# A recurrent attention and two MoE layers on one core: the first two chunks in a new order

## The chip, the cores and the metric

The kernel runs on one core of a Trainium2 chip. The metric is the device time of one execution in microseconds (us), taken as the median of several runs. TensorE is PE in the profile, VectorE DVE, ScalarE ACT, GpSimd POOL, and SP is the engine that issues the DMAs.

## The reference

The input is a recurrent attention with 4 x 8 heads, 768 steps and head size 40. For every step t and head, with a 40 x 40 state S:

```
y[t] = r[t] @ S
S    = S * w[t][:, None] - outer(S @ a[t], b[t]) + outer(v[t], k[t])
```

The result, 3072 tokens of 320, goes through two feed-forward layers: MoE 1 is `h = x @ w_in` (320 x 2048), `g = h * clip(h + 3, 0, 6) / 6`, `g @ w_out`; MoE 2 is `((x @ w_a) * (x @ w_b)) @ w_out` with 1536 columns. The MoE weights arrive as 64-bit floats, which the kernel converts to 32 bits on the chip.

## The kernel before, in words

**Attention** is done in 12 chunks of 64 steps, all 32 heads at once. A chunk j has a fixed chain. `prep_w`, `prep_kb` and `prep_a` scale the inputs by running products of w (a scan and a reciprocal per quarter, DVE). `op_a` forms the products of the chunk on PE. GpSimd then inverts small 32 x 32 triangles: `t_load` writes them to DRAM (`scr`) and fetches them as TA2 (`TA`), `t_start` does 31 elimination steps of two instructions (L517, L520) into TL, and `t_store` lets ACT turn TL into `tnt` (L528) and sends TL and tnt through DRAM (`n`) back as NY and into AB. From there PE goes on: `merge_y` (L547), `merge_z` (L559), `op_c` and `op_d`, `op_e`, `op_g`, `op_f`, which gives Y; Y goes through DRAM to `xt`, the input of MoE 1 for this chunk. ACT copies what PE leaves in PSUM, in four banks, after each of these.

**MoE 1** for a chunk is a `prep` (ACT casts xt to xh, L288, DVE takes the rest xl) and 16 steps, up 0 to 7 and down 0 to 7. An up is 16 matmuls (L309), then ACT relu into the tile g (L314), DVE multiply (L315), ACT cast gh (L130), DVE rest gl (L131). A down is 12 matmuls (L329 to L331). MoE 2 follows when all chunks are done and keeps PE busy to the end.

**The order** on every engine is the order in which the Python program issues the work. Each chunk j has a window: a list of attention steps of chunk j and preparations of chunks j + 1 and j + 2, and between them places where one MoE 1 step (`MOE_STEP`) or one weight conversion (`WEIGHT`) goes; the places are the index lists MOE and WEIGHTS. A step issues its instructions on all engines, its DMAs on SP's queue among them.

**The weights** of MoE 1 come in 34 pieces (18 of w_in, 16 of w_out, in the order in which up and down need them). A conversion is: DMA into a tile, one ACT scaling (L77), five DVE instructions (L78 to L86), one ACT cast (L261), one DVE subtraction (L263). While room is wide (four tiles, xt, xh, xl and GH, are lent to the conversion), `Interleaved.round` overlaps three pieces, each round takes one new piece. `op_e` takes GH back, with extra rounds until GH is free; the first `xt_move` ends the wide state with `flush`. After that a piece goes through alone, from tiles `ws` and `cv`; an up or down whose weights are not there converts them first (`need`).

**Before the windows** a prologue prepares chunks 0 and 1, runs `t_start(0)` and `t_start(1)` on GpSimd, some conversions, the transposes `turn(0)` and `turn(1)`, and `t_store(0)`. `prep_kb` of chunk 1 is on GpSimd there, ahead of `t_start(0)`, and the second half of `t_load(1)` (the fetch into TA2, which GpSimd must have finished reading) stands on SP's queue ahead of the loads of chunk 2 and of `t_store(0)`.

The tail after the windows runs what is left of MoE 1, two steps apart, and converts the first 15 pieces of MoE 2's weights between them, one after each step from the third on.

Of the kernel before, what the change touches and what calls it, by code (L numbers as in the profile page):

```python
# [21 lines left out]
NCH = S // C  # L22
# [14 lines left out]
WEIGHTS = {
    0: (0, 3, 6, 8, 10, 17, 18, 21, 22, 22, 26, 27),
    1: (1, 2, 4, 5, 10, 13, 16, 16, 33, 36)}
STORE_1 = 25  # L40
WEIGHTS_2, RANGE = 2, 7
# [53 lines left out]
def attention_and_moe(ctx, tc, t, flag):  # L95
# [44 lines left out]
    def words(src, dma):  # L140
        st = wk1.tile([128, 192, 2], I32, tag="ws", name="ws", bufs=3)[:, 0:src.shape[1]]
        dma.dma_start(out=st.rearrange("q c w -> q (c w)"), in_=src.bitcast(I32))
        return st

    def from_words(st):
        cv = wk1.tile([128, 2, 192], I32, tag="cv", name="cv2", bufs=2)[:, :, 0:st.shape[1]]
        return to_f32(nc, st, cv[:, 0], cv[:, 1], st[:, :, 1])

    class Converter:
# [5 lines left out]
        def ahead(self, most=2):  # L155
            while self.todo and len(self.loaded) < most:
                k, src, n, sink, c0 = self.todo.pop(0)
                w, begun = self.load(src, n, sink, c0)
                if w < n:
                    self.todo.insert(0, (k, src[:, w:n], n - w, sink, c0 + w))  # L160
                self.loaded.append((k, begun))

# [12 lines left out]
    class Interleaved(Converter):  # L175


        x = y = z = None

# [3 lines left out]
        def go(self, n=1):  # L183
            if not room["wide"]:
                return super().go(n)
            for _ in range(n):
                self.ahead()
                self.round()
                self.ahead()
# [30 lines left out]
    def load1(src, n, sink, c0):  # L220

        slot = None
        if room["wide"]:
            slot = room["free"].pop(0)
            room["live"].add(slot)
            if slot == "GH":
                st = GH.rearrange("q a p c -> q (a p c)")[:, 0:2 * n]
                sp.dma_start(out=st if not wide else st.bitcast(I32), in_=src.bitcast(I32) if wide else src)
                st = st.bitcast(I32).rearrange("q (c w) -> q c w", w=2) if wide else st
            else:  # L230
                st = stage_load(wk1, (slot, 0, 0, 0, 0, 1), src, n, sp)
        else:
            n = min(n, 192)
            st = words(src[:, 0:n], sp) if wide else stage_load(wk1, ("ws", 0, 0, 0, 0, 3), src[:, 0:n], n, sp)

        def steps():
            if not wide:
                yield from range(6)
                w = st
            elif slot:  # L240
                room["n"] += 1
                h = wk1.tile([128, n], I32, tag=("cv", "gh")[room["n"] % 2], name="cv_h", bufs=2)
                f32_steps(nc, st, h, h, h)[0]()
# [12 lines left out]
            yield  # L256
        return n, steps()

    def weight_pieces1():
# [32 lines left out]
    def moe1_stream(j):  # L292
# [5 lines left out]
        def up(i):  # L298
            conv1.need(0, (2 * i + 1) // 3)
            xh, xl = stt["x"]  # L300
# [62 lines left out]
    TLs = [a1.tile([128, 32, 16], F32, name=f"TL{i}") for i in range(2)]  # L363
    TT2 = a1.tile([128, 256], F32, name="TT2")
    KBTv = [x[:, 0:2 * NP * D].rearrange("q (a p d) -> q a p d", a=2, p=NP) for x in KBTs]
# [13 lines left out]
    def setup_first():  # L379
        for q, eng in ((32, ve), (96, gp)):  # L380
            eng.memset(raw[q:q + 32], 1.0)
            eng.memset(raw[q:q + 32].rearrange("q (p t) -> q p t", p=NP)[:, :, 0:1], 0.0)
        load_kb(0)
# [110 lines left out]

    def t_load(j, between=lambda: None):
        scr = dram.tile([2, 2, NP, 32, 32], F32, tag="scr", name="scr", bufs=2)
# [6 lines left out]
        between()  # L503
        for h in range(2):
            sp.dma_start(out=TA2[half(h)], in_=scr.rearrange("u a p s t -> (u a p) s t"))

# [14 lines left out]

    def t_store(j, between=lambda: None):
        TL = TLs[j % 2]
        tnt = wk1.tile([128, 16, 32], F32, tag="g", name="tnt", bufs=1)
        NY = py["NY"] = a2.tile([128, NP, 32], F32, tag="py", name="NY")
        n1 = dram.tile([2, 2, NP, 32, 32], F32, tag="n1", name="n1", bufs=2)
        z, AB = n2[j % 2], ABs[j % 2]
        ac.copy(out=tnt, in_=TL.rearrange("q t c -> q c t"))  # L528
        for h in range(2):
# [3 lines left out]
            sp.dma_start(out=z.rearrange("a p (c h) t -> (a p) c h t", h=2)[:, :, h, 32:64], in_=tnt[r + 32:r + 64])  # L533
        between()
# [160 lines left out]
    WEIGHT, MOE_STEP = "weight", "moe"  # L695

    def window(j):

# [9 lines left out]
        def pk(*ks):  # L708
# [3 lines left out]
            [(op_b, j, 0), (op_b, j, 1)]  # L712
            + on(nx2 and j, (load_w, j + 2)) + on(nx2, (load_a, j + 2)) + on(j > 1, (t_store, j))
            + on(ahead, (op_a, j + 1, 0), (idle,))
            + on(ahead, (op_a, j + 1, 1), (idle,), (t_load, j + 1), (t_start, j + 1)) + pw(0)
            + on(ahead, (op_kbt, j + 1, 0), (op_kbt, j + 1, 1)) + pw(1)
# [8 lines left out]
            + on(nx2, (prep_a, j + 2, gp), (prep_sq, j + 2)))  # L725
        if j < 2:
            steps = [x for x in steps if x is not WEIGHT]
        out = []
        for i, x in enumerate(steps + [None]):
            if j == 0 and i == STORE_1:  # L730
                out.append((t_store, 1, conv1.go))
            if j == 1 and i == 0:
                out.append((xt_move, 0))
            out += [WEIGHT] * WEIGHTS.get(j, ()).count(i) + [MOE_STEP] * MOE[j].count(i)
            if x is not None:
                out.append(x)
# [178 lines left out]
    with tc.manual_schedule():  # L915
# [4 lines left out]
        for k in range(4):  # L920
# [51 lines left out]

        for j in range(NCH):
            for f in window(j):
                if f == MOE_STEP:
# [253 lines left out]
```

## Time and profile before

| | |
|---|---|
| median of 3 runs | 1327.77 us (1323.69 to 1331.85) |
| profiled execution | 1324.79 us, its span 1323.0 us |
| mean granted PE clock | 0.940 |
| busy | PE 84%, DVE 58%, ACT 38%, POOL 28% |
| DMA | 97.59 MB, mean 74 GB/s |

A share is of the whole span. The span has three stages: up to about 200 us the preparation, chunk 0 and the conversions, with PE mostly idle; then one window after another, with MoE 1 steps between attention steps; from about 908 us MoE 2.

### The profile page before, as it was taken

How to read it: one execution, taken by the hardware profiler on the slowest of the kernel's cores; microseconds unless marked ns; L12 is line 12 of the kernel's file. 1: busy time of each engine (PE TensorE's matmuls, PEld its weight loads, DVE VectorE, ACT ScalarE, POOL GpSimd, SP SyncE). 2: the span in 40 equal slices, each digit the busy share in tenths (PEclk: the TensorE clock that was granted, in tenths of full speed). 3: DMA queues.
4: the chain of work that ended last, by engine and by line, in shares of the span. 5: the costliest groups of instructions: out<-in, count | busy, mean ns of one | idle time of the engine just before them, and what ended most of it. 6: DMA issues, size and time to landing. Idle time of an engine off the chain costs nothing.

```text
span 1323.0 us, 34883 instructions
## 1 busy us (share of the span) xinstructions
PE 1110.3 (84%) x14826; PEld 1013.2 (77%) x14826; DVE 771.6 (58%) x1371; ACT 504.5 (38%) x1087; POOL 375.0 (28%) x829
## 2 busy tenths in 40 slices
PE   1314438898989898989999999877999999999998
PEld 1214338798989898988988898866888888888886
DVE  7869777374646556473746243576665675675333
ACT  2224244344444544354544534233433332332221
POOL 4775007171817263553627250000000000000000
PEclk9999658998989898989999899989999999999999
DMA  6245351424151524333241412122220110110011
GB/s 174 70 119 129 95 130 49 100 63 119 39 140 36 122 60 98 83 86 91 66 112 51 100 40 54 62 75 89 85 70 27 35 42 27 34 43 11 32 41 50
DMA packets 166403, 97.59 MB, mean 74 GB/s; under 512 B 124672, under 2 KB 155520, under 8 KB 164224
## 3 DMA queue, kind: packets, MB, share of 16 engines
q1 hardware_dynamic: 166240, 95.29, 27.9%
q8 instruction: 118, 1.93, 0.6%
q14 instruction: 45, 0.37, 0.1%
HBM read 75.33 MB, written 19.92 MB: 72 GB/s over the span
## 4 chain that ended last, share of the span: by engine, by line
PE 63%; DVE 9%; ACT 9%; DMA 7%; POOL 5%; issue 4%; SPq 4%; ACTq 0%; DVEq 0%; POOLq 0%
PE att L847 20%; PE up L309 10%; PE dn L329 4%; PE dn L331 3%; PE dn L330 3%; PE ac L871 3%; PE ac L870 3%; PE ac L869 3%; POOL TL L520 2%; POOL TT L517 2%; DMA n<-tnt 2%; PE att L614 2%; PE att L637 2%; PE att L631 2%; PE att L588 2%
## 5 line engine op out<-in xcount | busy, mean ns | idle before, releaser
L517 POOL TENSOR_TENSOR TT<-TA,TL 128x126 f32<-128x126 f32 (+22 forms) x372 | 146.3, 393 | 340.1 <-DMA TA<-scr 311.8
L847 PE MATMUL att<-x2h,up 128*128 128x512 f32 x720 | 237.2, 394 | 0.2 <-ACT x2h L831 0.2
L847 PE MATMUL att<-x2l,up 128*128 128x512 f32 x432 | 170.4, 394 | 1.9 <-DVE x2l L832 1.9
L520 POOL TENSOR_TENSOR TL<-TL,TT 128x126 f32<-128x126 f32 (+22 forms) x372 | 156.8, 421 | 29.1
L315 DVE SCALAR_TENSOR_TENSOR up<-g,up 128x512 f32<-128x512 f32 x96 | 66.4, 691 | 156.3 <-ACT g L314 156.3
L847 PEld LDWEIGHTS att<-x2h,up 128*128 128x128 f32 x720 | 135.0, 188 | 29.2 <-ACT x2h L831 0.5
L329 PE MATMUL dn<-wo_h,gh 128*128 128x320 f32 x384 | 137.2, 357 | 21.0 <-ACT gh L130 21.0
L314 ACT ACTIVATE g<-up,bias 128x512 f32<-128x512 f32 x96 | 66.3, 691 | 192.6 <-PE up L309 126.5
L331 PE MATMUL dn<-wo_h,gl 128*128 128x320 f32 x384 | 128.9, 336 | 1.4 <-DVE gl L131 1.4
L330 PE MATMUL dn<-wo_l,gh 128*128 128x320 f32 x384 | 128.0, 333 | 0.0
L309 PE MATMUL up<-xh,wi_h 128*128 128x256 f32 x384 | 107.2, 301 | 3.1 <-ACT xh L288 3.1
L852 DVE TENSOR_TENSOR att<-att,asb 128x512 f32<-128x512 f32 x72 | 50.4, 700 | 97.9 <-PE att L847 79.3
L131 DVE TENSOR_TENSOR gl<-up,gh 128x512 fp32r<-128x512 f32 x96 | 66.4, 692 | 65.9 <-ACT gh L130 65.9
L309 PE MATMUL up<-xh,wi_l 128*128 128x256 f32 x384 | 101.7, 286 | 0.0
L329 PEld LDWEIGHTS dn<-wo_h,gh 128*128 128x128 f32 x384 | 80.8, 210 | 26.6 <-ACT gh L130 22.9
L130 ACT CAST gh<-up 128x512 fp32r<-128x512 f32 x96 | 56.3, 586 | 114.8 <-DVE up L315 110.8
L847 PEld LDWEIGHTS att<-x2l,up 128*128 128x128 f32 x432 | 81.0, 188 | 19.4 <-DVE x2l L832 3.5
L869 PE MATMUL ac<-dn,g2h 128*128 128x320 f32 x288 | 89.5, 311 | 0.0
L871 PE MATMUL ac<-dn,g2l 128*128 128x320 f32 x288 | 88.6, 308 | 0.1
L870 PE MATMUL ac<-dn,g2h 128*128 128x320 f32 x288 | 88.7, 308 | 0.0
L449 DVE RECIPROCAL rw<-W 128x256 f32<-128x256 f32 x48 | 84.2, 1753 | 4.3 <-ACT sq L459 1.7
L331 PEld LDWEIGHTS dn<-wo_h,gl 128*128 128x128 f32 x384 | 80.6, 210 | 4.0 <-DVE gl L131 4.0
(146 smaller groups left out, 2411.9 us busy)
## 6 DMA issues: line engine op xcount, KB each, us to landing
RV<-in_rve_dram SPq DMA_DIRECT2D x24, 320.0 KB
KB<-in_kbe_dram SPq DMA_DIRECT2D x22, 320.0 KB
TA<-scr SPq DMA_DIRECT2D x24, 256.0 KB
st<-in_w1i_dram SPq DMA_DIRECT2D x13, 384.0 KB
raw<-in_we_dram SPq DMA_DIRECT2D x24, 162.5 KB
LB<-in_ae_dram SPq DMA_DIRECT2D x24, 160.0 KB
VX<-in_vte_dram SPq DMA_DIRECT2D x24, 160.0 KB
yt<-Y SPq DMA_DIRECT2D x48, 80.0 KB
```

Source lines behind the costliest of these rows:

```text
L131: eng.tensor_tensor(out=lo, in0=src, in1=hi.bitcast(F32), op=ALU.subtract)
L309: mm(u[:, e], a_, b_, start=(n == 0), stop=(n == len(seq) - 1))
L329: mm(acc, gh[:, e, c0:c0 + 128], wo_h[:, m], start=(m == 0), stop=False)
L330: mm(acc, gh[:, e, c0:c0 + 128], wo_l[:, m], start=False, stop=False)
L331: mm(acc, gl[:, e, c0:c0 + 128], wo_h[:, m], start=False, stop=(m == 15))
L449: ve.reciprocal(out=rw, in_=w[:, :, 1:65])
L517: gp.tensor_tensor(out=tv, in0=TA2[:, u:u + 1, u + 1:32].rearrange("q a t -> q t a").to_broadcast([128, m, n]), in1=TL[:, u:u + 1, 0:n].to ...
L520: gp.tensor_tensor(out=TL[:, u + 1:32, 0:n], in0=TL[:, u + 1:32, 0:n], in1=tv, op=ALU.subtract)
L847: mm(u, a_, b_, start=(n == 0), stop=(n == len(seq) - 1))
L869: mm(acc, gh[:, sl], w[:, 0], start=(i == 0), stop=False)
L870: mm(acc, gh[:, sl], w[:, 1], start=False, stop=False)
L871: mm(acc, gl[:, sl], w[:, 0], start=False, stop=(i == BLOCK - 1))
```

## The change

Tables MOE and WEIGHTS lose their entries for windows 0 and 1, which are now written out by hand in `first_windows`; windows 2 to 11 keep their places. `t_load` and `t_store` are each cut in two. `t_start(0)` is issued right after `setup_rest`, `prep_kb` of chunk 1 goes to DVE, the prologue has six conversion rounds, two of them in each `turn`, where it had fourteen, and the fetch of chunk 1's triangles comes after `t_store(0)`. `tnt` is no longer the tile g of MoE 1 but the first half of TA2. Pieces of w_in have 344 columns instead of 384, and a piece is no longer cut at 192 columns when room is not wide. In that state `go` leaves a piece's last DVE instruction until the next piece (`settle`). Window 0 has no MoE step and four conversions; window 1 has 15 MoE places (a prep and 14 steps, where there were a prep and 10) and 12 conversion places.

```diff
-            n = min(n, 192)
-            st = words(src[:, 0:n], sp) if wide else stage_load(wk1, ("ws", 0, 0, 0, 0, 3), src[:, 0:n], n, sp)
+            st = words(src, sp) if wide else stage_load(wk1, ("ws", 0, 0, 0, 0, 2), src, n, sp)
...
 class Interleaved(Converter):
+        def settle(self):
+            for _ in self.rest or ():
+                pass
+            self.rest = None
         def go(self, n=1):
             for _ in range(n):
                 self.ahead()
+                if room["wide"]:
+                    self.round()
+                elif self.loaded:
+                    new = self.loaded.pop(0)[1]
+                    next(new)
+                    self.settle()
+                    self.rest = new
+                else:
+                    self.settle()
                 self.ahead()
...
+WCOLS = 344
...
-            c0, n = 384 * c, min(384, FF1 - 384 * c)
+            c0, n = WCOLS * c, min(WCOLS, FF1 - WCOLS * c)
...
-            conv1.need(0, (2 * i + 1) // 3)
+            conv1.need(0, (256 * i + 255) // WCOLS)
...
-        tnt = wk1.tile([128, 16, 32], F32, tag="g", name="tnt", bufs=1)
+        tnt = TA2[:, 0:16]
...
+    def t_in(j):
+        t_load(j)
+        t_fetch(j)
+    def t_out(j):
+        t_store(j)
+        t_place(j)
...
+        W, M = WEIGHT, MOE_STEP
+        yield [
+            (merge_y, 0), W, (merge_z, 0), (op_d, 0, 0), (op_d, 0, 1), (op_c, 0, 0), (op_c, 0, 1), W, (op_e, 0, 0),
+            (op_g, 0, 0), (op_g, 0, 1), (load_vt, 1), W, (op_f, 0, 0), (st_copy, 1), (op_e, 0, 1), W, (op_f, 0, 1),
+            (xt_move, 0), (load_rv, 1), (op_sd, 1, 0), (op_sd, 1, 1), (prep_w, 2, 0), (prep_kb, 2, 0), (prep_w, 2, 1),
+            (prep_kb, 2, 1), (op_b, 1, 0), (op_b, 1, 1)]
+        yield [
+            (t_store, 1), M, (t_place, 1), M, (prep_w, 2, 2), (prep_kb, 2, 2), M, (prep_w, 2, 3), (prep_kb, 2, 3),
+            (load_w, 3), (load_a, 3), (merge_y, 1), M, (prep_a, 2, gp), (merge_z, 1), M, (op_c, 1, 0), W, (op_c, 1, 1),
+            (op_d, 1, 0), (op_d, 1, 1), W, M, (op_a, 2, 0), W, (op_a, 2, 1), (t_in, 2), (t_start, 2), M, (op_g, 1, 0),
+            (op_g, 1, 1), (load_vt, 2), W, (op_e, 1, 0), M, (st_copy, 2), W, (op_f, 1, 0), M, (op_e, 1, 1), W, M,
+            (op_f, 1, 1), (xt_move, 1), W, (load_rv, 2), (op_sd, 2, 0), (op_sd, 2, 1), (op_kbt, 2, 0), (op_kbt, 2, 1),
+            M, (prep_w, 3, 0), (op_kbt, 2, 2), (op_kbt, 2, 3), (load_kb, 3), W, M, (prep_w, 3, 1), W, (prep_kb, 3, 0),
+            M, W, (prep_w, 3, 2), (prep_kb, 3, 1), W, M, (prep_w, 3, 3), (prep_kb, 3, 2), W, M, (prep_kb, 3, 3),
+            (prep_a, 3, gp), (prep_sq, 2), (prep_sq, 3)]
...
-        t_load(0)
+        t_in(0)
         setup_rest()
+        t_start(0)
         load_vt(0)
         for k in range(4):
             prep_w(1, k)
-            prep_kb(1, k, gp)
+            prep_kb(1, k)
             later.pop(0)()
         prep_a(1)
-        t_start(0)
         for hf in range(2):
             op_a(1, hf, later)
+            conv1.go()
             for _ in range(2):
-                conv1.go()
                 later.pop(0)()
+        t_load(1)
         def turn(j):
             for bk in range(4):
                 op_kbt(j, bk)
-                conv1.go()
-        t_load(1, lambda: turn(0))
-        t_start(1)
+                if bk % 2:
+                    conv1.go()
+        turn(0)
         load_w(2)
         load_kb(2)
         turn(1)
         load_rv(0)
+        op_b(0, 0)
+        op_b(0, 1)
+        load_a(2)
         prep_sq(0)
         prep_sq(1)
-        conv1.go()
-        t_store(0, conv1.go)
+        t_store(0)
+        t_fetch(1)
+        t_start(1)
+        t_place(0)
```

At the very start `load_kb(0)` also moves behind `load_w(0)` and `load_a(0)` on SP's queue.

## Rows read from the trace of the kernel before

**Rows 1.** The page, part 1: busy time, share of the span and instructions of each engine.
```profile
PE 1110.3 (84%) x14826; PEld 1013.2 (77%) x14826; DVE 771.6 (58%) x1371; ACT 504.5 (38%) x1087; POOL 375.0 (28%) x829
```
**Rows 2.** Windows: stretch, its length, busy time per engine, PEclk, DMA share, GB/s.
```profile
140.00:160.00 20.00, 8.47 (x197) 7.65 (x199) 14.36 (x36) 6.36 (x11) 0.00 (x0) 0.59 0.39 103
...
220.00:240.00 20.00, 20.00 (x454) 18.96 (x455) 11.83 (x18) 6.87 (x14) 15.36 (x31) 1.00 0.10 29
```
**Rows 3.** Timeline of POOL: start, duration, engine, line, operation, tiles, count, [idle before, releaser].
```profile
42.49 0.30 POOL L517 TENSOR_TENSOR TT<-TA,TL 128x31 f32<-128x31 f32 x1
...
79.41 0.22 POOL L520 TENSOR_TENSOR TL<-TL,TT 128x16 f32<-128x16 f32 x1
...
84.02 0.24 POOL L517 TENSOR_TENSOR TT<-TA,TL 128x31 f32<-128x31 f32 x1 [3.58 <-DMA TA<-scr]
...
202.17 0.38 POOL L517 TENSOR_TENSOR TT<-TA,TL 128x31 f32<-128x31 f32 x1 [68.31 <-DMA TA<-scr]
...
231.96 0.22 POOL L520 TENSOR_TENSOR TL<-TL,TT 128x16 f32<-128x16 f32 x1
```
**Rows 4.** Timeline of PE, merge_y of chunk 0 and of chunk 2.
```profile
111.22 1.91 PE L547 MATMUL att<-NY,AB 32*32 32x32 f32 x62 [1.26 <-DMA NY<-n]
...
262.74 1.92 PE L547 MATMUL att<-NY,AB 32*32 32x32 f32 x64
```
**Rows 5.** Timeline of SP: the triangles' fetch for chunks 0 and 1.
```profile
30.99 1.14 SPq L505 DMA_DIRECT2D TA<-scr  x2
...
79.36 1.10 SPq L505 DMA_DIRECT2D TA<-scr  x2
```
**Rows 6.** Timeline of ACT: two wide rounds begin, and chunk 0's tnt.
```profile
71.17 0.57 ACT L77 ACTIVATE cv_h<-st 128x384 f32<-128x384 f32 x1
...
74.67 0.50 ACT L77 ACTIVATE cv_h<-st 128x320 f32<-128x320 f32 x1
...
100.16 1.07 ACT L528 COPY tnt<-TL 128x512 f32<-128x512 f32 x1
```
**Rows 7.** Timeline of ACT: pieces alone, of 128 and of 256 columns, and up chains.
```profile
184.33 0.32 ACT L77 ACTIVATE cv<-ws 128x128 f32<-128x128 f32 x1
...
186.38 0.31 ACT L77 ACTIVATE cv<-ws 128x128 f32<-128x128 f32 x1
...
849.63 0.43 ACT L77 ACTIVATE cv<-ws 128x256 f32<-128x256 f32 x1
...
852.99 0.44 ACT L77 ACTIVATE cv<-ws 128x256 f32<-128x256 f32 x1
...
855.81 0.42 ACT L77 ACTIVATE cv<-ws 128x256 f32<-128x256 f32 x1
...
859.41 0.68 ACT L314 ACTIVATE g<-up,bias 128x512 f32<-128x512 f32 x1
860.86 0.59 ACT L130 CAST gh<-up 128x512 fp32r<-128x512 f32 x1 [0.76 <-DVE up L315]
...
907.37 0.59 ACT L130 CAST gh<-up 128x512 fp32r<-128x512 f32 x1 [0.76 <-DVE up L315]
```
**Rows 8.** Windows: from merge_z's last copy of chunk 1 to tnt of chunk 2.
```profile
213.36:247.15 33.79, 33.79 (x757) 32.02 (x757) 18.55 (x26) 16.68 (x36) 21.14 (x42) 0.98 0.16 45
```
**Rows 9.** Groups of DVE, 0 to 245 us: shapes, count, busy us, mean ns, idle before.
```profile
L449 DVE RECIPROCAL rw<-W 128x256 f32<-128x256 f32 x16 | 28.0, 1753 | 1.7 <-ACT sq L459 0.4
```
**Rows 10.** The chain that ended last: one up of 16 matmuls.
```profile
219.97 2.11 PE up L309 x16
```
**Rows 11.** Timeline of DVE: the same instruction of a piece, beside chunk 1's triangles and alone.
```profile
95.95 0.72 DVE L80 SCALAR_TENSOR_TENSOR cv_h<-cv_h,cv_p 128x320 int32<-128x320 int32 x1
...
150.60 0.48 DVE L80 SCALAR_TENSOR_TENSOR cv_h<-cv_h,cv_p 128x320 int32<-128x320 int32 x1
```
**Rows 12.** Waits of ACT, 311 to 325 us: us in total, times, longest.
```profile
ACT g L314 <- DMA n<-tnt: 7.5, 1, 7.5
```
**Rows 13.** Timeline of SP: the second NY load of chunk 2.
```profile
258.25 0.48 SPq L537 DMA_DIRECT2D NY<-n  x1
```

More of the change, by code (lines that the diff above doesn't have):

```diff
@@ L36 @@
     NCH - 1: (3, 3, 3, 3, 3, 4, 6, 11, 11, 13, 13, 13, 19, 20, 23, 23, 23)}
[L37 to L40, printed above, removed]
+WCOLS = 344
 WEIGHTS_2, RANGE = 2, 7
@@ L140, in words @@
     def words(src, dma):
-        st = wk1.tile([128, 192, 2], I32, tag="ws", name="ws", bufs=3)[:, 0:src.shape[1]]
+        st = wk1.tile([128, WCOLS, 2], I32, tag="ws", name="ws", bufs=2)[:, 0:src.shape[1]]
         dma.dma_start(out=st.rearrange("q c w -> q (c w)"), in_=src.bitcast(I32))
@@ L145, in from_words @@
     def from_words(st):
-        cv = wk1.tile([128, 2, 192], I32, tag="cv", name="cv2", bufs=2)[:, :, 0:st.shape[1]]
-        return to_f32(nc, st, cv[:, 0], cv[:, 1], st[:, :, 1])
+        h = wk1.tile([128, WCOLS], I32, tag="cv", name="cv2", bufs=2)[:, 0:st.shape[1]]
+        return to_f32(nc, st, h, h, st[:, :, 1])
     class Converter:
@@ L157, in ahead @@
                 k, src, n, sink, c0 = self.todo.pop(0)
[L158 to L161, printed above, removed]
+                self.loaded.append((k, self.load(src, n, sink, c0)))
         def go(self, n=1):
@@ L175, in attention_and_moe, with need @@
     class Interleaved(Converter):
-        x = y = z = None
+        x = y = z = rest = None
+        def settle(self):
+            for _ in self.rest or ():
+                pass
+            self.rest = None
+        def need(self, side, last):
+            super().need(side, last)
+            self.settle()
         def ahead(self):
@@ L183, in go @@
         def go(self, n=1):
-            if not room["wide"]:
-                return super().go(n)
             for _ in range(n):
                 self.ahead()
-                self.round()
+                if room["wide"]:
[6 more added lines that the diff above has]
+                else:
+                    self.settle()
                 self.ahead()
@@ L256, in steps @@
             yield
-        return n, steps()
+        return steps()
     def weight_pieces1():
@@ L363, in attention_and_moe @@
     TLs = [a1.tile([128, 32, 16], F32, name=f"TL{i}") for i in range(2)]
-    TT2 = a1.tile([128, 256], F32, name="TT2")
+    TT2 = a1.tile([128, 136], F32, name="TT2")
     KBTv = [x[:, 0:2 * NP * D].rearrange("q (a p d) -> q a p d", a=2, p=NP) for x in KBTs]
@@ L382, in setup_first @@
             eng.memset(raw[q:q + 32].rearrange("q (p t) -> q p t", p=NP)[:, :, 0:1], 0.0)
-        load_kb(0)
         load_w(0)
@@ L389, in setup_first @@
         load_a(0)
+        load_kb(0)
         for q in (32, 96):
@@ L456, in square @@
     def square(src, scale, acc):
+        conv1.settle()
         tag, bufs = ("g", 1) if room["wide"] else ("cv", 2)
@@ L491, in op_a, with t_load @@
             masked() if later is None else later.append(masked)
-    def t_load(j, between=lambda: None):
-        scr = dram.tile([2, 2, NP, 32, 32], F32, tag="scr", name="scr", bufs=2)
+    def t_load(j):
+        scr = py["scr"] = dram.tile([2, 2, NP, 32, 32], F32, tag="scr", name="scr", bufs=2)
         AB = ABs[j % 2]
@@ L502, in t_load, with t_fetch @@
                              in_=AB[r0:r0 + 32, :, 32 * sub:32 * sub + 32])
-        between()
+    def t_fetch(j):
         for h in range(2):
-            sp.dma_start(out=TA2[half(h)], in_=scr.rearrange("u a p s t -> (u a p) s t"))
+            sp.dma_start(out=TA2[half(h)], in_=py["scr"].rearrange("u a p s t -> (u a p) s t"))
+    def t_in(j):
+        t_load(j)
+        t_fetch(j)
     def t_start(j):
@@ L520, in t_start, with t_store @@
             gp.tensor_tensor(out=TL[:, u + 1:32, 0:n], in0=TL[:, u + 1:32, 0:n], in1=tv, op=ALU.subtract)
-    def t_store(j, between=lambda: None):
+    def t_store(j):
         TL = TLs[j % 2]
-        tnt = wk1.tile([128, 16, 32], F32, tag="g", name="tnt", bufs=1)
-        NY = py["NY"] = a2.tile([128, NP, 32], F32, tag="py", name="NY")
-        n1 = dram.tile([2, 2, NP, 32, 32], F32, tag="n1", name="n1", bufs=2)
-        z, AB = n2[j % 2], ABs[j % 2]
+        tnt = TA2[:, 0:16]
+        n1 = py["n1"] = dram.tile([2, 2, NP, 32, 32], F32, tag="n1", name="n1", bufs=2)
+        z = n2[j % 2]
         ac.copy(out=tnt, in_=TL.rearrange("q t c -> q c t"))
@@ L533, in t_store, with t_place @@
             sp.dma_start(out=z.rearrange("a p (c h) t -> (a p) c h t", h=2)[:, :, h, 32:64], in_=tnt[r + 32:r + 64])
-        between()
+    def t_place(j):
+        NY = py["NY"] = a2.tile([128, NP, 32], F32, tag="py", name="NY")
+        n1, z, AB = py["n1"], n2[j % 2], ABs[j % 2]
         for ab in range(2):
@@ L695, in attention_and_moe, with first_windows @@
     WEIGHT, MOE_STEP = "weight", "moe"
+    def first_windows():
+        W, M = WEIGHT, MOE_STEP
[13 more added lines that the diff above has]
+            (prep_a, 3, gp), (prep_sq, 2), (prep_sq, 3)]
     def window(j):
@@ L712, in window @@
             [(op_b, j, 0), (op_b, j, 1)]
-            + on(nx2 and j, (load_w, j + 2)) + on(nx2, (load_a, j + 2)) + on(j > 1, (t_store, j))
+            + on(nx2 and j, (load_w, j + 2)) + on(nx2, (load_a, j + 2)) + [(t_out, j)]
             + on(ahead, (op_a, j + 1, 0), (idle,))
-            + on(ahead, (op_a, j + 1, 1), (idle,), (t_load, j + 1), (t_start, j + 1)) + pw(0)
+            + on(ahead, (op_a, j + 1, 1), (idle,), (t_in, j + 1), (t_start, j + 1)) + pw(0)
             + on(ahead, (op_kbt, j + 1, 0), (op_kbt, j + 1, 1)) + pw(1)
@@ L725, in window @@
             + on(nx2, (prep_a, j + 2, gp), (prep_sq, j + 2)))
-        if j < 2:
-            steps = [x for x in steps if x is not WEIGHT]
         out = []
         for i, x in enumerate(steps + [None]):
[L730 to L735, printed above, removed]
+            out += [MOE_STEP] * MOE[j].count(i)
+            if x is not None and x is not WEIGHT:
                 out.append(x)
@@ L971, in moe_step @@
                 mq.pop(0)()
-        for j in range(NCH):
-            for f in window(j):
+        windows = list(first_windows()) + [window(j) for j in range(2, NCH)]
+        for j, steps in enumerate(windows):
+            for f in steps:
                 if f == MOE_STEP:
@@ L980, in attention_and_moe @@
                 elif f == WEIGHT:
-                    if conv1.todo or conv1.loaded or room["wide"]:
+                    if conv1.todo or conv1.loaded or conv1.rest or room["wide"]:
                         conv1.go()
@@ L984, in attention_and_moe @@
                     f[0](*f[1:])
+        conv1.settle()
         at.close()
```

2 lines of the change are left out of this document (removed).

## The prediction

> **What bounds the kernel now.** I read the page first: over the span PE is the busiest engine, at 84% [rows 1], but a share over three stages says little. The windows by stage come next: at 220 to 240 us PE is busy for all 20 us, at 140 to 160 us for 8.47 [rows 2]. So what can be won lies ahead of about 200 us, and a start-up that ends x us earlier moves everything behind it by x. As the mark of its end I take merge_y of chunk 2 (262.74 [rows 4]): from there on both kernels issue the same lists, and by then MoE 1 has done 14 steps. The timelines of GpSimd, SP and ACT then show the start-up's order: chunk 0's triangles run from 42.49 to 79.63, chunk 1's only start at 84.02 [rows 3], and chunk 0's merge_y stands at 111.22 [rows 4].
>
> **Chunk 0 comes sooner.** The fetch of chunk 0's triangles was issued by 32.13 [rows 5]. The fetch for chunk 1 took 3.56 us from the last issue (80.46) to the first elimination step (84.02) [rows 3, 5], so chunk 0's landed at about 35.7, while GpSimd was still scaling KB of chunk 1. With that work on VectorE the triangles start at 35. Their length was 37.1 us beside conversions and 30.0 us in window 1 [rows 3]; I take 35, since six rounds still lie beside them, and keep both ends. They end at 70.
>
> The Trainium skill (GPSIMD Engine Reference, Key points) says that GpSimd shares its SBUF interfaces with VectorE and suffers from VectorE instructions with two SBUF inputs. By it the length stays 37.1 and the sum below is 2 us more; the trace has both lengths.
>
> From tnt to merge_y it was 11.1 us (100.16 [rows 6] to 111.22). Now the fetch for chunk 1 stands between `t_store(0)` and `t_place(0)` on SP, and must wait until the transfers have read tnt, which now lies in TA2: I add 1.5 (bounds 0 and 4). Merge_y of chunk 0 is at 82.6, 28.6 us earlier. Chunk 1's triangles start about 12 us behind chunk 0's end and finish near 115, ahead of their use. Moving KB of chunk 1 to VectorE costs four short multiplications in front of op_a(1); conversions are what waits behind them. The new DMA order at the start leaves the same bytes ahead of the first product: nothing, within 2 us either way.
>
> **Window 0.** Each round takes a new piece: six in the prologue, four in this window, and two more in op_e, because GH was reloaded and must be emptied; the flush takes the one loaded. So 13 pieces go through wide, and **21 are left**. VectorE sets the length: ten rounds, the flush included, at 3.5 us (71.17 to 74.67 [rows 6]) are 35; two quarters of prep_w and prep_kb, each a reciprocal of 1.75 [rows 9] and some 1.4 more, 6; masks, state and Y about 6; waits for merge_y and merge_z 4. That is 51, so tnt of chunk 1 at about 134. Then again 11 to merge_y, and about 12 for merge_y, merge_z, ACT's copies and the first two ups, on the same engines: the first piece that goes alone starts at **157** (bounds 149 and 165).
>
> **Window 1 is where the change loses.** A piece alone is a chain: ACT scaling, five VectorE instructions, ACT cast, and only then ACT's next scaling. Start to start that took 2.05 us for 128 columns and 2.82 for 256 [rows 7], 0.6 per 100 columns: 3.35 for 344, 3.2 for 320, 3.26 on average. That nothing hides this chain the tail of before shows: from 849.63 to 907.96 it has 15 pieces of 2.82 (or less) and 8 ups of 2.04 (relu at 859.41 to the cast's end at 861.45), 58.6 in sum against 58.3 measured [rows 7]. Window 1 now is such a stretch:
> - 21 pieces at 3.26: 68.5. Twelve places hold ten of them; eleven are forced by ups 2, 4, 5 and 6 (2, 1, 4 and 4).
> - the ACT-VectorE chains of ups 2 to 7: 6 x 2.04 = 12.2.
> - those four ups wait for their weights, so their own PE time comes on top: 4 x (2.11 [rows 10] + 0.5 for the last subtraction) = 10.4.
> - ACT's other work up to tnt of chunk 2: the stretch of before had 16.68 us busy [rows 8], four ups of 1.27 in it, so 11.6; less a square that lies ahead, and with the copies of op_a and op_kbt of chunk 2, a square and a cast that lay elsewhere: 16.5.
> - VectorE work for which ACT's next instruction stands: four quarters of prep_w and prep_kb 11, state and mask 3: 14.
>
> Sum 121.6. Chunk 2's triangles lie beside about seven of the pieces; the same VectorE instruction took 0.72 beside triangles and 0.48 alone [rows 11], about 1 us a piece for five: 5 more, with the overlap partly on ACT's time (bounds 0 and 9). Tnt of chunk 2 is done at 157 + 126.6 = 283.6, and merge_y, 10 us after tnt's end as for chunk 0, at **293.5**, against 262.74: **30.8 later**. MoE 1 has then done 18 steps, four more.
>
> **The four steps** come back in the tail: it then has 13 pieces and six ups behind its first piece, so 2 x 2.82 + 2 x 2.04 = 9.7 less; two pieces move into MoE 2, where VectorE has room. I take 9 (bounds 5 and 10).
>
> **TA2 for tnt.** In each window ACT stood 7.5 us at its relu until the transfers had read tnt from g [rows 12]; that goes. But what stands next? Merge_y needs NY. For chunk 2 its last load was issued by 258.73 [rows 13]; it landed after that and, with the 3.56 us of the larger fetch of the triangles as the most, before 262.3, and PE came at 262.74: 0.4 to 4 to win, some 1.5 (nearer the long end, since a quarter of the bytes still goes through DRAM). On the other side, the four extra steps put the prep of the next chunk at the end of the window, where ACT must wait for xt before the copies that lead to tnt. I take 0, with -1.5 and +0.7 per window as bounds, ten windows: -15 and +7.
>
> **Sum:** 30.8 - 9 + 0 = +21.8. On the profiled execution, 1324.79 with its 1.8 us around the span, that is 1346.6. The median is 3.0 higher than this execution, and the runs lie 8 us apart; I name 1347.
>
> **Rivals.**
> 1. *The forecast:* the chain of pieces and ups in window 1 sets the start, 1335 to 1359. Chance 0.5.
> 2. *Faster: the pieces overlap after all.* If ACT and VectorE run ahead of one another in window 1, only VectorE's own work counts there. It decides if a piece's place costs 2.6 us (six instructions, the longer ones 0.48 alone [rows 11]) instead of 3.26, and the ups hide behind pieces: -13.7 - 12.2 - 10.4 and no contention, -5, so merge_y of chunk 2 at about 252, 10.6 earlier than before, and with the four steps 1305. For it: the last subtraction is now put off behind the next piece, and preparations stand between some pieces. Against it: the tail's sum [rows 7]. Chance 0.19.
> 3. *The windows pay for the loss:* ACT's 7.5 us free in each window give the full 1.5 us ten times: 1332. For it: the gap before chunk 2's merge_y; against it: the later tnt. Chance 0.21.
> 4. *Slower still:* window 1's ups come in short bursts, as PE's work did at 140 to 160 us, where the granted clock was 0.59 [rows 2], mostly the lower level, 1.2 GHz, after PE had been idle more than half of the time. Then four forced ups cost 2.11 more each, and the attention's products as much again: +15, 1362. Chance 0.1. The Trainium skill (TensorE: Matmul & The Clock Gate, HAM oscillation) describes such bursts between waits falling back to the lower clock; the row agrees.
>
> That the new order does not do what it says, chunk 0's triangles held until 42 by their fetch, would put 7 us on rival 1 and stays inside its range.
>
> **Numbers.** About 1%, 13 us, is what can be told from no change. Faster is rival 2 and little else: 0.2. Same is rival 3 and the low end of the forecast: 0.27. Slower is the rest: 0.53. The range 1312 to 1362 leaves out most of rival 2 and half of rival 4; the forecast's own is 1335 to 1359.
>
> **What would show it.** GpSimd's first elimination at about 35 and merge_y of chunk 0 at about 83. First up of MoE 1 near 137. In window 1 from 157 on: 21 pieces of about 3.3 us on ACT, PE mostly waiting for ACT or VectorE, merge_y of chunk 2 near 293. No wait of ACT at L314 for the transfer of tnt. If merge_y of chunk 2 comes before 263, the chain was no chain and rival 2 holds; if it comes at 293 and the time is no longer, the windows gave it back.

## The result and the profile after

The changed kernel took 1346.17 us, median of 4 runs (1341.21 to 1347.85), against 1329.41 us for the kernel before on the same chip: ratio 1.0126, 95% interval 1.0082 to 1.017. It is slower by about 17 us; the forecast was slower, 1347, made of the profiled execution before and 21.8 us. Its profiled execution took 1346.49 us, span 1344.7; before 1324.79 and 1323.0, so 21.7 us between the spans.

The page's first part hardly changes: PE's busy time is 1% more, DVE's 1% less [rows 1].

```profile
PE 1121.0 (83%) x14826; PEld 1020.8 (76%) x14826; DVE 766.6 (57%) x1363; ACT 505.6 (38%) x1083; POOL 366.5 (27%) x825
```

The stages tell more. Windows of the changed kernel (stretch, length, busy time of PE, PEld, DVE, ACT, POOL, then PEclk, DMA share, GB/s):

```profile
60.00:80.00 20.00, 3.73 (x64) 3.61 (x64) 8.27 (x17) 7.54 (x20) 8.57 (x23) 1.00 0.71 171
80.00:100.00 20.00, 11.66 (x329) 10.90 (x330) 3.50 (x6) 7.54 (x15) 12.91 (x34) 1.00 0.36 72
140.00:160.00 20.00, 11.46 (x173) 10.39 (x171) 10.45 (x14) 7.33 (x15) 5.43 (x5) 0.76 0.43 103
220.00:240.00 20.00, 8.98 (x44) 7.90 (x44) 12.40 (x26) 5.87 (x14) 3.65 (x10) 0.57 0.41 109
240.00:260.00 20.00, 1.12 (x3) 0.79 (x3) 16.20 (x33) 4.97 (x12) 0.00 (x0) 0.60 0.30 84
```

The first two stretches in the kernel before:

```profile
60.00:80.00 20.00, 6.74 (x76) 5.49 (x76) 18.87 (x35) 7.40 (x23) 17.41 (x35) 1.00 0.35 89
80.00:100.00 20.00, 0.00 (x0) 0.00 (x0) 8.10 (x15) 5.08 (x12) 13.81 (x36) 1.00 0.61 164
```

Where PE had worked all 20 us [rows 2], from 220 to 240, it now works 9, and from 240 to 260 it works 1.1. And VectorE, on which the weights wait, is busy for 11.8 of the 40 us from 60 to 100, where it had been busy for 27.0. These two holes are the change: work was taken out of VectorE's hole and came up in PE's.

GpSimd's rows and merge_y of chunks 0 and 2, which answer to [rows 3] and [rows 4]:

```profile
35.79 0.24 POOL L530 TENSOR_TENSOR TT<-TA,TL 128x31 f32<-128x31 f32 x1 [10.82 <-DMA TA<-scr]
...
69.13 0.22 POOL L533 TENSOR_TENSOR TL<-TL,TT 128x16 f32<-128x16 f32 x1
...
84.51 0.24 POOL L530 TENSOR_TENSOR TT<-TA,TL 128x31 f32<-128x31 f32 x1 [14.35 <-DMA TA<-scr]
...
193.27 0.24 POOL L530 TENSOR_TENSOR TT<-TA,TL 128x31 f32<-128x31 f32 x1 [37.14 <-DMA TA<-scr]
```
```profile
86.60 1.91 PE L566 MATMUL att<-NY,AB 32*32 32x32 f32 x62 [1.19 <-DMA NY<-n]
...
292.51 1.30 PE L566 MATMUL att<-NY,AB 32*32 32x32 f32 x62 [1.43 <-DMA NY<-n]
```

Chunk 0 comes 24.6 us sooner (111.22 to 86.60) and chunk 2 29.8 us later (262.74 to 292.51). In between lie 21 pieces that go alone. ACT's timeline in window 1, where four follow one another, and the relu of two ups that had to wait for their weights:

```profile
235.93 0.69 ACT L321 ACTIVATE g<-up,bias 128x512 f32<-128x512 f32 x1 [3.57 <-PE up L316]
...
249.68 0.48 ACT L72 ACTIVATE cv<-ws 128x320 f32<-128x320 f32 x1
...
252.86 0.49 ACT L72 ACTIVATE cv<-ws 128x328 f32<-128x328 f32 x1
...
256.17 0.49 ACT L72 ACTIVATE cv<-ws 128x328 f32<-128x328 f32 x1
...
259.49 0.52 ACT L72 ACTIVATE cv<-ws 128x328 f32<-128x328 f32 x1
...
264.69 0.69 ACT L321 ACTIVATE g<-up,bias 128x512 f32<-128x512 f32 x1 [1.85 <-PE up L316]
```

A piece starts 3.18 to 3.32 us after the one before it. PE stands for the weights meanwhile, and what is left of an up after its last piece keeps ACT waiting for 1.85 us or, at the lower granted clock, 3.57. The waits from 158 to 292 us (us in total, times, longest), of ACT for VectorE's part of a conversion and of PE for weights:

```profile
ACT wo_h L268 <- DVE cv L81: 31.3, 10, 4.7
ACT wi_h L268 <- DVE cv L81: 19.1, 7, 4.5
...
ACT wi_t L268 <- DVE cv L81: 9.8, 4, 2.5
```
```profile
PE up L316 <- ACT wi_h L268: 32.5, 4, 16.2
PE up L316 <- DVE wi_l L270: 16.9, 6, 3.5
```

ACT stands 60.2 us in these waits, one for each of the 21 pieces, and PE 49.4.

From merge_y of chunk 2 the 21.7 us split into +29.8 at that mark, -2.9 in the windows to merge_y of chunk 11 (542.5 us before, 539.6 after), and -5.1 from there to the end (517.7 and 512.6).

### The profile page after: what moved, and what is told of

Same layout as the page of the kernel before. It is cut to its first block, busy times and chain, and to the rows that moved or that the text cites. A ratio compares the mean times of both kernels' runs of the same rounds, so it can differ in the third digit from the quotient of the medians.

```text
span 1344.7 us, 34822 instructions
## 1 busy us (share of the span) xinstructions
PE 1121.0 (83%) x14826; PEld 1020.8 (76%) x14826; DVE 766.6 (57%) x1363; ACT 505.6 (38%) x1083; POOL 366.5 (27%) x825
## 4 chain that ended last, share of the span: by engine, by line
PE 51%; DVE 17%; DMA 12%; ACT 11%; issue 5%; SPq 4%; POOL 0%; DVEq 0%; ACTq 0%; POOLq 0%
PE att L878 19%; PE up L316 8%; PE dn L336 3%; PE ac L902 3%; PE ac L901 3%; PE ac L900 3%; DMA KB<-in_kbe_dram 3%; DMA xt<-yt 2%; DVE rw L456 2%; PE dn L337 2%; PE dn L338 2%; PE att L633 2%; DMA n<-TA 2%; DVE up L322 2%; DMA NY<-n 2%
## 5 line engine op out<-in xcount | busy, mean ns | idle before, releaser
L316 PE MATMUL up<-xh,wi_h 128*128 128x256 f32 x384 | 111.1, 309 | 48.4 <-ACT wi_h L268 32.5
L316 PE MATMUL up<-xh,wi_l 128*128 128x256 f32 x384 | 106.6, 298 | 16.9 <-DVE wi_l L270 16.9
L316 PEld LDWEIGHTS up<-xh,wi_h 128*128 128x128 f32 x384 | 77.7, 202 | 51.5 <-ACT wi_h L268 33.4
L125 ACT CAST gh<-up 128x512 fp32r<-128x512 f32 x96 | 56.2, 586 | 158.8 <-DVE up L322 123.1
L316 PEld LDWEIGHTS up<-xh,wi_l 128*128 128x128 f32 x384 | 77.7, 202 | 18.7 <-DVE wi_l L270 18.7
```

The source lines that it names most:

```text
L316: mm(u[:, e], a_, b_, start=(n == 0), stop=(n == len(seq) - 1))
```

## Experiments

Each is told with its ratio to the kernel before, timed on the same chip; marks are the main burst of merge_y in the profile, and each profile is of one execution.

**The changed kernel once more**, unchanged; below it is called the control.

> The changed kernel as it is, as a control on the same chip as the others. From merge_y of chunk 2 to that of chunk 11 it took 539.6 us in its profile, where the kernels with the same lists took 543 to 548. Theory A (that was a quick execution, TA2 is worth nothing in the windows): 1346 to 1351, ratio to the kernel before 1.013 to 1.017. Theory B (TA2 is worth 0.8 us a window): 1344 to 1347, ratio 1.011 to 1.013.

1349.3 us, ratio 1.0163 (1.013 to 1.0195), as theory A had it. Merge_y of chunk 2 stands at 292.8, and the windows take 543.8 us. Nine kernels with the same lists from window 2 on (this one, the changed one and seven below) took 539 to 546 us there, so a difference of a few us in that stretch between two profiles says nothing.

**tnt in TA2, alone.**

```diff
-        tnt = wk1.tile([128, 16, 32], F32, tag="g", name="tnt", bufs=1)
+        tnt = TA2[:, 0:16] if j else wk1.tile([128, 16, 32], F32, tag="g", name="tnt", bufs=1)
```

> The kernel before, with the turned triangles (tnt) of chunks 1 to 11 in the first half of TA2 and nothing else changed. Theory A (first reading of the two traces): ACT's 7.5 us wait at its relu holds back the MoE work behind it, and the period from tnt to tnt, 60.9 us before and 60.1 after, is TA2's doing: nine to ten windows at 0.8 us, 7 to 8 us faster than before, about 1321. Theory B (the prediction's term): ACT's wait is hidden, the transfers of NY come at the same time, so 0, 1328 to 1330; the shorter period of the changed kernel then comes from MoE 1 being four steps further. Either way ACT no longer waits for a transfer of tnt.

1329.28 us, ratio 0.9988 (0.997 to 1.0006): theory B. ACT's wait for tnt's transfer (56.2 us in nine waits before) is gone, and it was not idle time off the path either: in the kernel before, PE stood 27.6 us in eight waits for a PSUM bank that ACT had not emptied. The waits of PE from merge_y of chunk 2 to chunk 11 (us in total, times, longest), before and with tnt in TA2:

```profile
PE att L569 <- ACT KBT L572: 27.6, 8, 4.3
```
```profile
PE att L547 <- DMA NY<-n: 17.2, 13, 2.2
PE dn L329 <- ACT gh L130: 17.1, 8, 4.9
```

The 27.6 us went, and 17.2 for NY and 17.1 for gh came in their place.

**tnt back in g, in the changed kernel** (chunks 2 to 11).

```diff
-        tnt = TA2[:, 0:16]
+        tnt = wk1.tile([128, 16, 32], F32, tag="g", name="tnt", bufs=1) if j > 1 else TA2[:, 0:16]
```

> The changed kernel, with tnt of chunks 2 to 11 back in the tile g of MoE 1 and nothing else changed. Theory A: the period of the windows goes back from 60.1 to 60.9 us and merge_y of chunk 2, now 9.5 us behind its tnt, stands up to 5 us later: 7 to 12 us slower than the changed kernel, about 1354. Theory B: no difference, 1346, and periods of 60.1 us stay.

1354.37 us, ratio 1.0186 (1.0158 to 1.0214), against 1.0126 and 1.0163 for the changed kernel, whose intervals overlap with it. Merge_y of chunk 2 does not move (291.4); its windows took 547.7 us, just above the nine. Whether TA2 is worth a few us in the changed kernel stays open; 7 to 12, theory A, is not shown.

**Pieces alone without the conversion on VectorE.** The kernel leaves out five instructions of each piece, so these weights are not the real ones.

```diff
-        return to_f32(nc, st, h, h, st[:, :, 1])
+        f32_steps(nc, st, h, h, st[:, :, 1])[0]()
+        return h.bitcast(F32)
```

> The changed kernel, but the pieces that go alone (window 1) leave out the five VectorE instructions of the conversion: scaling and cast on ACT and the last subtraction stay, so the weights of these pieces are not the real ones. Theory A (the chain ACT, VectorE, ACT of 21 pieces at 3.3 us sets window 1): a piece costs between 1.0 us (ACT alone) and 2.0 (its 350 KB at the 170 GB/s that the first slice of the span shows), so window 1 loses 27 to 48 us: merge_y of chunk 2 at 244 to 265 where it stands at 291, and 1300 to 1320 in all. Theory B (chunk 2's triangles and PE's own work at a low clock set window 1): less than 10 us, merge_y of chunk 2 beyond 281, above 1336.

1318.02 us in one run. Merge_y of chunk 2 at 260.0, 32.5 us sooner: theory A, nearer its lower end. A window row of the changed kernel from the first such piece on, this kernel's row up to merge_y of chunk 2, and one of ACT's waits in it:

```profile
158.00:281.00 123.00, 64.25 (x946) 56.96 (x945) 85.60 (x165) 41.05 (x94) 31.76 (x67) 0.67 0.32 85
```
```profile
158.00:260.00 102.00, 73.04 (x1078) 65.45 (x1077) 47.39 (x71) 50.06 (x109) 29.65 (x67) 0.74 0.43 113
```
```profile
208.32 0.51 ACT L72 ACTIVATE cv<-ws 128x344 f32<-128x344 f32 x1 [3.97 <-DMA ws<-in_w1i_dram]
```

VectorE is busy 47 of 102 us where it had 85.6 of the 123 from 158 to 281; now the pieces wait for their loads, 14.7 us in six waits. So the pieces' work on VectorE held window 1, and behind it stands, among other things, the loading.

**Six more wide rounds before the windows**, behind `t_place(0)`.

```diff
         t_place(0)
+        conv1.go(6)
```

> The changed kernel with six more wide conversion rounds behind t_place(0), in the 22 us (68.3 to 90.3) in which VectorE waits for chunk 0's triangles to come back. All the work is done, only earlier. Theory A (the loss is that the rounds were taken from this stretch and became pieces that go alone): six pieces fewer in window 1 at 3.3 us, 20 less and up to 3 more for the waits of the ups; merge_y of chunk 0 stays within 3 us of 86.6; merge_y of chunk 2 at about 270, 1326 in all, level with the kernel before or a little faster. Theory B (the rounds hold up ACT's copies and the loads of the pieces hold up the transfers of the triangles): merge_y of chunk 0 8 to 12 us later, and only half is won, 1336.

1332.46 us, ratio 1.0012 (0.9988 to 1.0035), merge_y of chunk 2 at 273.6. That is nearer theory A (about 270, level with the kernel before), but the way there was partly theory B's. The third round's load stood on SP behind `t_place(0)`, and ACT stood for it ahead of chunk 0's copy (timeline of ACT):

```profile
89.49 0.51 ACT L72 ACTIVATE cv_h<-st 128x344 f32<-128x344 f32 x1 [13.88 <-DMA st<-in_w1i_dram]
...
102.16 1.18 ACT L570 COPY NY<-att 32x512 f32<-32x512 f32 x2
```

The copy came 13.6 us late (88.55 in the changed kernel) and tnt of chunk 1 15.5; the 13 pieces alone that were left, eight fewer, gave back 34.5.

**Four rounds between the transfers**, with their loads on SP ahead of what blocks it.

```diff
         t_store(0)
+        conv1.go(2)
         t_fetch(1)
         t_start(1)
+        conv1.go()
         t_place(0)
+        conv1.go()
```

> The changed kernel with four more wide rounds: two between t_store(0) and the fetch for chunk 1, one behind t_start(1), one behind t_place(0), so that their loads stand on SP's queue ahead of what blocks it, where the six rounds of the run before had a load that landed 13.9 us late and held ACT's copy behind merge_y of chunk 0 until 102. Theory A: copy of merge_y of chunk 0 at 88 to 92, window 0 as long as in the changed kernel, 4 to 5 pieces fewer alone at 3.3 to 4.3 us: merge_y of chunk 2 at 272 to 279 (292.5), 1327 to 1333 in all. Theory B (loads hold up the transfers of the triangles, or ACT is held by a load again): copy of merge_y of chunk 0 beyond 95, merge_y of chunk 2 beyond 282.

1331.96 us, ratio 1.0039 (1.0017 to 1.0061): theory A. ACT's copy and merge_y of chunk 2:

```profile
90.32 1.18 ACT L570 COPY NY<-att 32x512 f32<-32x512 f32 x2 [4.65 <-PE att L566]
```
```profile
275.14 1.31 PE L566 MATMUL att<-NY,AB 32*32 32x32 f32 x62 [1.51 <-DMA NY<-n]
```

The same conversions, four rounds earlier, bring merge_y of chunk 2 17.4 us forward, 4.4 us a round, and the time by as much against the control: most of the loss. Tnt of chunk 1 comes only 0.8 us later (136.43 for 135.65).

**The next piece's scaling ahead of this one's cast.** For this it has more tiles and pieces of 320 columns, three pieces more in all; only the order is shown here.

```diff
...
+                    if self.ready:
+                        next(self.ready[1])
                     next(new)
                     self.settle()
                     self.rest = new
```

> The changed kernel, but where pieces go alone, the next piece's scaling is issued on ACT ahead of this one's cast, so that VectorE finds it ready. For this there are three tiles ws and three cv, pieces of w_in have 320 columns (37 pieces in all, so about 24 left for window 1), GpSimd has one TL, and a square uses the tile g. Theory A (the handing over ACT, VectorE, ACT is what a piece's 3.3 us hold beyond VectorE's own 2.6): 24 x 2.6 = 62 where there were 21 x 3.3 = 69, and scalings no longer stand between ups: merge_y of chunk 2 at 281 to 287 (292.5 before the edit), 1335 to 1341 in all. Theory B (the pieces wait for their loads or for the ups, whatever ACT's order): periods of 3.2 us and more stay, three more pieces, 1346 to 1352.

1347.18 us, ratio 1.0156 (1.0124 to 1.0187), level with the control. Pieces that follow one another do come sooner (timeline of ACT):

```profile
238.65 0.50 ACT L72 ACTIVATE cv<-ws 128x320 f32<-128x320 f32 x1
...
241.35 0.50 ACT L72 ACTIVATE cv<-ws 128x320 f32<-128x320 f32 x1
...
243.81 0.50 ACT L72 ACTIVATE cv<-ws 128x320 f32<-128x320 f32 x1
```

That is 2.5 to 2.7 us in place of 3.2 to 3.3, so the handing over is real; but merge_y of chunk 2 at 287.2 is at theory A's late end, and the median shows nothing of it: it lies in theory B's range.

**The last piece of the tail later.** In the tail PE waited for the rows of x2d that MoE 2 starts with. Before, and in the changed kernel, whose SP queue is shown too:

```profile
909.44 0.88 PE L828 MATMUL att<-ident,xin 128*128 128x128 f32 x6 [3.51 <-DMA xin<-x2d]
```
```profile
922.27 5.33 SPq L803 DMA_DIRECT2D ws<-in_w2o_dram  x2
927.65 0.43 SPq L845 DMA_DIRECT2D xin<-x2d  x1
```
```profile
930.82 1.54 PE L859 MATMUL att<-ident,xin 128*128 128x128 f32 x6 [11.51 <-DMA xin<-x2d]
```

The load of the rows stood behind a load of weights that waited for its tile.

```diff
-            if n > WEIGHTS_2:
+            if n > WEIGHTS_2 and len(mq) > 2:
```

> The changed kernel without the last conversion place of the tail (the 13th piece of MoE 2's weights goes to MoE 2). In the changed kernel SP's queue stood from 922.3 to 927.6 at that piece's load, the load of the second half of MoE 2's first rows came behind it, and PE waited 11.5 us for it (3.5 before the change). Theory A (the tail's expected gain was lost there): the load at about 922.7, PE's transposes at about 926 in place of 930.8, 4 to 5 us less in all, 1342. Theory B (the piece is forced later on a waiting PE): PE's wait shrinks, but MoE 2 takes about 3 us more, 1345 to 1346.

1351.83 us, ratio 1.018 (1.0151 to 1.0209): not faster than the control. PE's waits from 920 us on (us in total, times, longest) and a window:

```profile
PE att L859 <- DMA xin<-x2d: 6.4, 1, 6.4
PE ac L900 <- ACT dn L125: 4.1, 1, 4.1
PE att L878 <- DVE up L130: 2.1, 1, 2.1
```
```profile
953.00:973.00 20.00, 15.54 (x68) 13.03 (x68) 11.28 (x30) 6.12 (x16) 0.00 (x0) 0.83 0.27 79
```

The wait for the rows is 5.1 us shorter, but PE then stands 6.2 us for the piece, and the granted clock is 0.83 in the window that holds the longer of these two waits: from the second rows' cast to the end this execution took 423.0 us against 412.9 in the control, and 409.8 to 416.1 in all other profiles. The cost is larger than theory B had it.

**The rows' load ahead of the weights' load**, on top of the four rounds. `go` gets a flag by which the last one loads no further piece; that comes behind `load_x(1)`.

```diff
-                w2.go(BLOCK - 1)
+                w2.go(BLOCK - 1, len(mq) > 2)
...
         load_x(1)
+        w2.ahead()
```

> The kernel with rounds between, and the tail's last load of MoE 2's weights issued behind the load of the second half of MoE 2's first rows instead of ahead of it; all 13 pieces stay where they are. In the kernel with the last piece later the rows came 4.9 us sooner, but PE then waited 6.2 us for the piece's parts at a lower granted clock. Theory A (only SP's order cost the 8 us more of waiting for the rows): PE's wait for them falls from 11.5 to about 6.5 us, and that stays won: 4 to 5 us less than with rounds between, 1327 to 1328. Theory B (the weights' load that comes later is missed in MoE 2): won and lost again, 1332.

1323.71 us, ratio 0.9988 (0.9969 to 1.0007); with the four rounds alone it was 1.0039. Theory A: PE's wait is 6.47, and from merge_y of chunk 11 to the end it takes 507.5 us where it took 512.2.

```profile
911.32 1.54 PE L860 MATMUL att<-ident,xin 128*128 128x128 f32 x6 [6.47 <-DMA xin<-x2d]
```

**Four steps out of the windows**, on top of the four rounds: windows 3, 5, 7 and 9 without their last MoE place, so that the tail has its 21 steps again.

> The kernel with rounds between (four more wide rounds), and windows 3, 5, 7 and 9 without their last MoE place, so that the four steps that window 1 does early are taken from windows in which PE is busy, and the tail is as long as in the kernel before (21 steps). Theory A (the four steps are worth little in the tail, where the pieces of MoE 2's weights hide PE, but their full PE time in a window): two ups and two downs are 18.7 us of PE, less the 3 to 5 us that the shorter tail had won: 10 to 15 us less than with rounds between, 1317 to 1322, faster than the kernel before by 0.4 to 0.8%. Theory B (a window's length is set by the chunk's chain of products, triangles and transfers, not by PE's load): nothing in the windows and the tail 3 to 5 us longer, 1335 to 1337.

1327.61 us, ratio 1.0017 (0.9988 to 1.0046), between the theories and not told apart from the four rounds alone (1.0039). The windows of the four rounds alone and of this kernel, from merge_y of chunk 2 to that of chunk 11:

```profile
275.14:814.45 539.31, 507.33 (x9516) 475.82 (x9516) 285.65 (x388) 251.17 (x523) 259.84 (x598) 0.97 0.34 83
```
```profile
276.29:806.23 529.94, 494.92 (x9461) 465.80 (x9461) 282.96 (x383) 248.89 (x519) 261.82 (x598) 0.96 0.36 85
```

They take 529.9 us for 539.3 (529.2 in the kernel that comes next), and the tail 517.1 for 512.2. The 18.7 us that was expected of PE is too much: the durations of the matmuls of two ups and two downs add up to 17.5 us, but they overlap. From start to next start an up takes 2.11 us [rows 10] and a down 1.9, so the four are about 8 us, and PE's busy time fell by 12.4. So the windows gave back the four steps in full, as theory A had it; the size of the term was wrong, and the tail took half of the gain back.

**Rounds between, steps moved and scaling ahead.**

> Rounds between, four steps moved, and the next piece's scaling issued ahead of the cast (as in the kernel with scaling ahead, which reached merge_y of chunk 2 5.5 us sooner). Theory A: the three add up as far as they lie in different stretches: merge_y of chunk 2 at 268 to 272 (275 with rounds between), and 3 to 6 us less than four steps moved: 1313 to 1319. Theory B (fewer pieces alone leave nothing for the scaling to hide, and three more pieces of 320 columns cost as much): level with four steps moved.

1329.27 us, ratio 1.0032 (1.0009 to 1.0054), merge_y of chunk 2 at 278.3: theory B. With fewer pieces alone, scaling ahead gains nothing.

**Chunk 2's preparation in the hole**, on top of rows ahead of load.

```diff
         conv1.go()
+        for k in range(2):
+            prep_w(2, k)
+            prep_kb(2, k)
...
-            (merge_z, 0), (op_d, 0, 0), (op_d, 0, 1),
+            (merge_z, 0), (prep_w, 2, 2), (prep_kb, 2, 2, nc.vector, False),
+            (op_d, 0, 0), (prep_w, 2, 3), (prep_kb, 2, 3, nc.vector, False), (op_d, 0, 1),
```

> The kernel with rows ahead of load (which has the four rounds between), and chunk 2's prep_w and prep_kb earlier: two quarters behind the last of the four rounds, two between merge_z of chunk 0 and op_d, where VectorE still stood 5.4 and 6.8 us with no piece at hand. Their inputs are loaded by then, so nothing is added to SP's queue; they leave the end of window 0 and the first steps of window 1. Theory A (VectorE's order sets the start up to merge_y of chunk 2): two quarters of 3.1 us off the way to tnt of chunk 1 (137.5 to about 131), two off window 1; merge_y of chunk 2 at 264 to 268 (276.1), 9 to 12 us less than rows ahead of load: 1312 to 1316, faster than the kernel before. Theory B (the ups and pieces in window 1 wait for one another whatever comes before them, and the squares hold up ACT's copies of chunk 0): merge_y of chunk 2 not before 272, 1320 to 1325.

1319.78 us (12 runs), ratio 0.9968 (0.995 to 0.9986): the one kernel of these that beats the one before, by 0.3%. It is not told apart from rows ahead of load alone (0.9988, 0.9969 to 1.0007), and the 1312 to 1316 of theory A was not reached. A window of rows ahead of load, then this kernel's and its merge_y of chunk 2:

```profile
80.00:100.00 20.00, 9.36 (x215) 8.67 (x216) 7.62 (x18) 7.51 (x14) 11.56 (x28) 1.00 0.57 141
```
```profile
80.00:100.00 20.00, 9.76 (x239) 9.07 (x240) 19.26 (x26) 8.35 (x19) 14.36 (x32) 1.00 0.42 97
```
```profile
267.85 1.31 PE L570 MATMUL att<-NY,AB 32*32 32x32 f32 x62 [1.79 <-DMA NY<-n]
```

VectorE is busy 19.3 of the 20 us in which it had been busy 7.6 (3.5 in the changed kernel), and merge_y of chunk 2 comes 8.3 us sooner than with rows ahead of load (276.1), in theory A's range (264 to 268). Tnt of chunk 1 hardly moved (135.9 from 137.5, for the 131 expected), so it was mostly window 1 that became shorter.

## Why the prediction was right, point by point

- **Chunk 0 sooner.** Triangles 35.79 to 69.35, length 33.6 (said: 35 to 70, 35). By the Trainium skill (GPSIMD Engine Reference, Key points), as I had read it, the length would have stayed 37.1; the measured 33.6 lies midway between the two lengths of [rows 3], so it decides nothing. From tnt (69.81) to merge_y it was 16.8 us where I had 12.6 with a bound of 15.1: SP's issues of `t_store(0)` run to 78.6, one of them 4.2 us long, and only then come the fetch and `t_place(0)`. Merge_y at 86.6 for 82.6. This term was too small, and its bound too.
- **Window 0.** 13 pieces wide, 21 left; 50 us to tnt of chunk 1 (51); first piece alone at 158.1 (157). Right, but that it is right to 1 us is luck: a start 4.0 later met a way from there that was 2.9 shorter.
- **Window 1.** 21 pieces at 3.2 to 3.4 us where nothing stood between. From the first to the end of tnt of chunk 2 124.3 us (126.6), merge_y of chunk 2 at 292.5 (293.5). By ACT's timeline the 124.3 are 80.0 of pieces from scaling to the end of the cast, with VectorE's other work and the slowing beside the triangles inside, 15.7 of the six ups, 11.0 of waits for the PE time of the four that were held up, and 17.7 of the rest; the sum had 87.5 (68.5 + 14 + 5), 12.2, 10.4 and 16.5. Leaving VectorE's part out took 32.5 us away, giving rounds back 4.4 each: the mechanism is shown, not only the sum. Rival 4's low clock was there too: behind two of the four ups ACT waited 3.6 to 3.7 us for PE, behind the other two 1.85, so 3.5 us in all and not 15. The Trainium skill (TensorE: Matmul & The Clock Gate, HAM oscillation) describes such falls between waits; the traces agree.
- **The four steps.** I took 9 with 5 as the lower bound; 5.1 came, 4.4 in the control. This is the term that was mis-sized most. The 9.7 behind the number was there: from the first piece to the end of the pieces it takes 48.3 us for 58.2. But 2.8 were lost ahead of it, between merge_y of chunk 11 and the first piece: PE had waited 3.1 us for NY just before, and the granted clock was 0.64 for the first 7.9 us, for 1.00 before the change. And 2.0 were lost behind it, where the rows' load stood behind the weights' load. I had not followed SP's queue to the end of the tail.
- **TA2.** I took 0 and named NY as what stands next. Alone it is -0.1% (-0.3 to +0.1), with 17.2 us of waits for NY; that gh would take as much I had not named. What PE lost to ACT's wait (27.6 us) I had not seen either.
- **The sum.** 29.8 - 2.9 - 5.1 = 21.7 (rounded) for 30.8 - 0 - 9 = 21.8. It is that close because a tail that gave 3.9 less than said met a start 1 shorter and windows that, in this execution, were 3 quicker; the control has 30.1 + 1.3 - 4.4 = 27.0. The 1347 itself came from the profiled execution; I had written that the median lay 3.0 above it and then did not add them. Between the medians it was 16.8 in the result and 21.8 in the control. The mechanism was right, the last digit luck.
- **Rivals.** Rival 2 (pieces overlap) falls: VectorE's own 2.5 to 2.7 shows only if the order is changed for it, and even then not in the time. Rival 3 falls with TA2 alone, and in the changed kernel the windows gave 2.9 us, in the control none, where it wanted 15.

## What to carry to other kernels

A conversion that overlaps with others costs little where its busiest engine would have stood: four rounds in VectorE's hole put tnt of chunk 1 off by 0.8 us. Alone, a piece costs the sum of its steps on both engines, and everything that waits for it: 4.4 us for each of these rounds. Before work is moved out of a stretch, look whether its engine will have anything else there: VectorE's hole at 60 to 100 us was left when rounds went out of the prologue. It could be filled with conversions whose loads stood ahead of what blocked SP's queue (17.4 us at merge_y of chunk 2), and then with work whose inputs were already on the chip (8.3 us more); conversions whose loads came behind the block lost 15.5 us on the way. Steps done early are worth what the place that no longer has to do them is bound by, and the queue behind that place has to be read to its end.

## What the runs showed of the hardware that I had not expected

A wait can cost more than its length through the clock. With the last piece later, 6.2 us of waits go with 10 us more in MoE 2. The two waits end at 946.80 and 961.76 us, and windows of that kernel show the granted clock behind them:

```profile
946.00:950.00 4.00, 3.20 (x8) 2.52 (x9) 0.42 (x1) 0.88 (x2) 0.00 (x0) 0.58 0.17 45
950.00:955.00 5.00, 4.61 (x27) 3.88 (x26) 3.28 (x8) 1.59 (x4) 0.00 (x0) 1.00 0.00 0
...
960.00:965.00 5.00, 3.24 (x12) 3.17 (x13) 2.38 (x7) 0.75 (x2) 0.00 (x0) 0.53 0.19 54
```

The control has 1.00 from 960 to 980. This is one execution; the medians of the two kernels are 2.5 us apart, within their intervals.

Waits of 3.1 us for NY in window 11 of the changed kernel end at merge_y's main burst, and matmuls at the lower level follow. The same stretch behind merge_y of chunk 11, before and in the changed kernel:

```profile
805.25:813.00 7.75, 7.75 (x203) 7.33 (x202) 2.30 (x5) 4.41 (x8) 0.00 (x0) 1.00 0.14 47
```
```profile
832.09:840.00 7.91, 7.91 (x150) 7.58 (x151) 0.82 (x2) 2.59 (x5) 0.00 (x0) 0.64 0.15 47
```

Not every short wait does this: before the change PE waited 1.9 us up to 802.86, in window 10, and the granted clock stayed at 1.00.
